# Three DMA pairs for two attention heads, and five loads moved ahead at the start of the output stage

## The chip, the cores and the metric

The kernel runs on one core of a Trainium2 chip. The metric is the device time of one execution in microseconds (us). Engines are named as in the profile: PE is TensorE, DVE is VectorE, ACT is ScalarE, POOL is GpSimd, SP is SyncE, which here only issues DMAs. Instructions run in order on each engine; between engines they wait for semaphores.

## The reference

Two blocks read the same input `x` (2048 tokens by 1024), and a gate mixes them:

```python
qkv = (x @ wqkv).reshape(B, S, 3, H, Dh).transpose(2, 0, 3, 1, 4)   # H = 32 heads, Dh = 32
scores = einsum("bhqd,bhkd->bhqk", q, k) * Dh ** -0.5
a = einsum("bhqk,bhkd->bhqd", softmax(scores), v).transpose(0, 2, 1, 3).reshape(B, S, D) @ wo

q = einsum("nd,dhc->nhc", x, w_q)              # 32 router heads, 2 x 128 wide
e = 8 * argmax(q[..., :128] @ k1.T) + argmax(q[..., 128:] @ k2.T)
b = sum over heads of gelu(x . u[e]) * v[e]    # K = 1: the softmax over one score is 1

g = sigmoid((x * gate_w).sum(-1))
out = g * a + (1 - g) * b
```

All of it is float32. The kernel splits many operands into a high and a low part and adds three products, so that a matmul keeps the precision.

## The kernel before, in words

The work stands in one hand-ordered program. Up to about 630 us come the projections, the router and the values. Then the 32 heads follow each other, and from about 1620 us the output product with `wo`.

**Attention.** A head `h` is 16 tiles of keys (`kt`). For each, PE makes scores for 128 keys and 2048 queries in a ring of seven PSUM banks (L1292), ACT writes their exponentials to an SBUF tile `P[h, kt]` of 128 x 2048 (L1301), and PE multiplies it with the values into `o` (L1313). The rows' sums for the softmax are formed apart: `presum` adds up the exponential tiles on DVE into `ACC[h]` (L1354, two instructions of half a tile each). Some tiles come in pairs: `accumulate` (L1343) adds one tile of a pair to the other with a DMA on POOL's queue, and `add_pair` and `merge` add the pair's sum to `ACC[h]` on DVE, the first one around the start of the next head. `pairs_of(h)` says which tiles are pairs: two pairs, (0, 2) and (8, 10), or three, with (4, 6) between. A head with three pairs has one addition less on DVE and one DMA of 1 MB more.

`p_tile` chooses the buffer of each exponential tile from the buffers that are left (13 places at first, 11 from the middle of head 19, 10 from head 29; two of them are kept for the end), always the one that its table `until` holds free earliest. That table gives the first tile of a pair 16 tiles of time, the second 10, and other tiles 5. ACT waits where the last reader of the buffer is not done. When the pairs change, the choice of buffers changes for every tile behind them. The copy of a finished head's output is `osb` (`finish`, L1390), one per head.

**The last head and the output.** The output is the product of the normed attention output with `wo`, 256 tokens (a chunk) at a time: `OD` holds the raw output of each group of four heads, `RD` the factors (gate over row sum), both in DRAM. `load_o` brings a chunk's part of `OD` into `V`, `load_rb` its factors, in a tile `P8` or `P9` (`rb` for chunk 0); `load_chunk` does both. Chunks 0 and 1 are done plainly (`wo_mm`, L1572); chunks 2 to 7 by `unit(n)`, a scheme of seven products of halves (`Halves.product`, L155). Its right-hand combinations of `wo`, T1 to T4, were made earlier and lie in DRAM as `TD`, a high and a low part of 1 MB each: `t0h`, `t0l` (T1), `t1h`, `t1l` (T2), `t2h`, `t2l` (T3), `t3h`, `t3l` (T4). `load_t(i, p, places)` loads part `p` of T(i+1). The DRAM tensor `t3l` is not the SBUF tile `t3l`: the tile holds `t2l`.

The last head's row sum goes a long way: PE sums (`sm`), ACT copies (`ssb`), SP stores it (`smd`), SP loads it spread out (`rr`), DVE takes the reciprocal (`norm_r`), SP stores it to `RD` (`rd`), and only then the last group's factors can be loaded: those of chunk 0 (`rb<-rd`), chunk 1 (`P<-rd`, small), chunk 2 and 3 (`P<-rd`, 256 KB each). All of these and the T loads stand on SP's queue; chunk 1's first part (`V<-od` x7, `P<-rd` x4) and `at` stand on POOL's. Between them PE does chunk 0 by `wo_mm(pa, 0, [kc])` for kc = 1 to 6, while `split_hi` and `split_lo` split `wo` out of `wo_raw0` to `wo_raw3`; the T parts are loaded over these tiles when they have been read.

Of the kernel before, what the change touches and what calls it, by code (L numbers as in the profile page):

```python
# [11 lines left out]
F32R = mybir.dt.float32r  # L12
# [5 lines left out]
S = 2048  # L18
D = 1024
H = 32  # L20
KC = D // 128
# [11 lines left out]
def gated_mha_peer_kernel(ctx, tc, xT, wqkv, wv, wo, wq, k12, ug, v, out):  # L33
# [46 lines left out]
    def dma(dst, src, queue=nc.sync):  # L80
        a, b = (ap.bitcast(F32) if ap.dtype == F32R else ap for ap in (dst, src))
        return queue.dma_start(a, b)  # L82
# [1068 lines left out]
    def pairs_of(h):  # L1151
        if h == H - 1:
            return (2, 4), (2, 6)
        if (h % 4 and h < 26) or h == H - 4:
            return (0, 2), (8, 10)
        return (0, 2), (4, 6), (8, 10)

# [63 lines left out]
    def raw_wo(kc):  # L1221
        i, j = divmod((kc - 1) % KC, 2)
        return wo_raw[i][:, j]
# [121 lines left out]
    def pair(h, i):  # L1345
        return P[h, pairs_of(h)[i][0]]
# [40 lines left out]
    def finish(h):  # L1387
        g, j = divmod(h, 4)
        o = wk.tile([128, 512], F32, name="osb")
        nc.scalar.activation(o, O.pop(h), AF.Copy)  # L1390
        dma(OD[g][32 * j:32 * j + 32, :].rearrange("d (q s) -> q d s", q=NQ), o)


    def norm_sums(h, ps, heads=1):
        g, j = divmod(h, 4)
        o = wk.tile([128, 512], F32, name="ssb")
        ins = nc.scalar.activation(o, ps, AF.Copy)
        for i in range(heads):
            dma(SMD[g][j + i:j + i + 1, :].rearrange("o (q s) -> (o q) s", q=NQ), o[32 // heads * i::32, :])
        return ins  # L1400


    def load_r(g):
        R[g] = wk.tile([128, 128], F32, name="rr", bufs=1)
        if g == G - 1:
            dma(R[g][:, :64], SMD[g].rearrange("j (b m) -> (j b) m", m=64))
        else:
            dma(R[g].rearrange("p (r m) -> p r m", r=2), SED[g][:2].rearrange("r j (b m) -> (j b) r m", m=64),
                nc.gpsimd if g == G - 2 else nc.sync)
# [13 lines left out]
    def load_o(n, k0, k1, queue=nc.sync):  # L1423
        if k0 == 0:
            OC[n] = vpool.tile([128, KC, W], F32, name="V")
        for kc in range(k0, k1):
            dma(OC[n][:, kc, :], OD[kc][:, n * W:(n + 1) * W], queue)

    def load_rb(n, k0, k1, js=range(4), queue=nc.sync):
        if k0 == 0 and js[0] == 0:  # L1430
            RB[n] = rb0 if n == 0 else wk.tile([128, KC, W], F32, name=f"P{8 + n % 2}", bufs=1)
        for j in js:
            src = RD[k0:k1, j:j + 1, n * W:(n + 1) * W].rearrange("g j s -> j g s")
            dma(RB[n][32 * j:32 * j + 32, k0:k1, :], src.to_broadcast([32, k1 - k0, W]), queue)

    def load_chunk(n, k0, k1, queue=nc.sync):
        load_o(n, k0, k1, queue)
        load_rb(n, k0, k1, queue=queue)
# [114 lines left out]
    fin = Pool("fin")  # L1553
# [41 lines left out]
    def split_hi(kc):  # L1595
        nc.scalar.activation(woh[kc], raw_wo(kc), AF.Copy)
        if kc < KC - 1:
            o = OC[0][:, kc, :]
            nc.vector.tensor_mul(o, o, RB[0][:, kc, :])
            nc.scalar.activation(OH[0][:, kc, :], o, AF.Copy)  # L1600

    def split_lo(kc):
        nc.vector.tensor_tensor(out=wol[kc], in0=raw_wo(kc),
                                in1=woh[kc].bitcast(F32), op=OP.subtract)
        if kc < KC - 1:
            nc.vector.tensor_tensor(out=OL[0][:, kc, :], in0=OC[0][:, kc, :],
                                    in1=OH[0][:, kc, :].bitcast(F32), op=OP.subtract)
# [3 lines left out]
    def load_t(i, p, part):  # L1611

        src, m = TD[i][p], HC // len(part)
        for j, place in enumerate(part):
            dma(place, src[:, m * j:m * j + m, :].rearrange("p k m -> p (k m)"))
        ht.b.setdefault(f"T{i + 1}", {})[p] = [place[:, k * 512:(k + 1) * 512] for place in part for k in range(m)]

    def raw_place(i):
        return [keep.tile([128, S], F32R, name=f"wo_raw{i}")]
# [18 lines left out]
    def split_o(n, k0, k1):  # L1638
        o = OC[n][:, k0:k1, :]
        nc.vector.tensor_mul(o, o, RB[n][:, k0:k1, :])  # L1640
        split(OH[n][:, k0:k1, :], OL[n][:, k0:k1, :], o)
# [7 lines left out]

    t3l = fin.tile([128, S], F32R, name="t3l")
    finish(H - 1)
    sm = pso.tile([128, 512], F32, name="o")
    list(rowsum(sm, *(P[H - 1, NT - i] for i in (1, 2)), ACC.pop(H - 1)))
# [4 lines left out]
    for kc in range(1, KC - 1):  # L1660
        split_hi(kc + 1)
        if kc == 1:
            norm_sums(H - 1, sm)
            load_r(G - 1)
            pso.close()
        split_lo(kc)
        wo_mm(pa, 0, [kc], False, False)
    split_lo(KC - 1)
# [1 line left out]
    norm_r(G - 1)  # L1670
    for n in range(2):
        load_chunk(n, KC - 1, KC)
        load_t(0, n, raw_place(n))
    load_t(2, 1, [t3l])
    OH[1] = zp.tile([128, KC, W], F32R, name="z1")
    OL[1] = wk.tile([128, KC, W], F32R, name="acc")
    split_o(1, 0, HC)
    load_chunk(2, 0, KC)
    load_t(1, 0, raw_place(2))
    ps_odd = Pool("ps_odd", space=PSUM)  # L1680
    for (i, half), ps in pa.items():
# [148 lines left out]
```

## Time and profile before

| what | us |
|---|---|
| runs: median (lowest to highest of 3) | 1808.1 (1807.08 to 1811.17) |
| the profiled execution | 1806.74 |
| its span in the profile | 1805.0 |
| PE busy over the span | 1795.3 (99%) |
| DVE busy | 1499.4 (83%) |
| ACT busy | 1217.7 (67%) |
| POOL busy | 273.6 (15%) |

A profile's busy time of PE includes ends that are modelled: matmuls overlap, and a PE that waits a little for ACT in every round still reads as full. The share of one engine over the whole span mixes stages with different limits, so the stages are looked at apart. In a row of the order of time stand start, duration, engine, line, operation, tiles (out<-in), their shapes and the number of instructions, and in brackets the idle time before them with what ended it. Engine names with a q are of the engine's queue: `SPq` is a DMA being issued, not being moved.

### The profile page before, as it was taken

What the parts mean: (1) busy time and instruction counts of PE and PEld (TensorE: products, weight loads), DVE (VectorE), ACT (ScalarE), POOL (GpSimd) and SP (SyncE); (2) the same over time, 40 slices, a digit from 0 to 9 for tenths busy, and PEclk for the clock granted to TensorE, in tenths of its full rate; (3) what the DMA queues carried; (4) which work ended last, traced back from release to release, by engine and by line L of the source; (5) the groups of instructions that cost most, each with busy time, mean ns of one, the idle gap of its engine ahead of it and who ended that gap; (6) DMA issues with size and microseconds to landing.
All of it is one profiled execution on the core that took longest, in us unless ns stands there. A gap on an engine that the chain in (4) does not pass through costs nothing.

```text
span 1805.0 us, 27885 instructions
## 1 busy us (share of the span) xinstructions
PE 1795.3 (99%) x10567; PEld 1135.2 (63%) x10567; DVE 1499.4 (83%) x1675; ACT 1217.7 (67%) x1608; POOL 273.6 (15%) x339
## 2 busy tenths in 40 slices
PE   9999999999999999999999999999999999999999
PEld 7777777788888754555454555454554545547787
DVE  7868776358987789999999999998999989895584
ACT  4434321211233399999999999999999999992221
POOL 0222000026401201111111111111111121211000
PEclk9999999999999999999999999999999999999999
DMA  6888888723238688899899999998998998977861
GB/s 241 237 285 255 276 258 294 261 79 107 82 125 278 227 200 173 173 186 205 175 209 189 197 201 192 194 189 178 196 213 180 206 218 191 201 153 204 282 180 65
DMA packets 132241, 359.04 MB, mean 199 GB/s; under 512 B 18484, under 2 KB 58564, under 8 KB 106936
## 3 DMA queue, kind: packets, MB, share of 16 engines
q1 hardware_dynamic: 90040, 190.61, 36.1%
q0 software_dynamic: 21904, 130.69, 35.9%
q10 hardware_dynamic: 20160, 35.92, 7.0%
q8 instruction: 84, 1.38, 0.3%
q14 instruction: 53, 0.43, 0.1%
HBM read 176.25 MB, written 86.09 MB: 145 GB/s over the span
## 4 chain that ended last, share of the span: by engine, by line
PE 95%; DMA 3%; SPq 1%; ACT 0%; DVE 0%; issue 0%; ACTq 0%; DVEq 0%
PE ring L1292 29%; PE o L1313 26%; PE bk L155 13%; PE bk L711 10%; PE pa L155 5%; PE bk L758 5%; PE bk L926 2%; PE bk L311 2%; PE bk L491 1%; PE bk L395 1%; DMA at<-atd 1%; SPq L82 1%; PE pa L1579 1%; DMA woh<-t3h 0%; DMA wraw<-in_wqkv 0%; DMA V<-od 0%
## 5 line engine op out<-in xcount | busy, mean ns | idle before, releaser
L1301 ACT ACTIVATE P<-ring 128x512 f32<-128x512 f32 (+3 forms) x991 | 812.9, 944 | 14.9 <-PE ring L1292 8.6
L1354 DVE TENSOR_TENSOR acc<-acc,P 128x1024 f32<-128x1024 f32 x424 | 488.3, 1217 | 18.9 <-ACT P L1301 18.9
L1313 PE MATMUL o<-P,V 128*32 128x512 f32 (+1 forms) x4072 | 417.5, 527 | 0.0
L1292 PE MATMUL ring<-Q,K 98*128 98x512 f32 x1024 | 269.0, 406 | 0.0
L1292 PE MATMUL ring<-z,z 98*128 98x512 f32 x1020 | 268.3, 406 | 0.1
L1292 PEld LDWEIGHTS ring<-Q,K 98*128 98x128 f32 x1024 | 182.8, 188 | 117.7 <-issue 37.0
L1292 PEld LDWEIGHTS ring<-z,z 98*128 98x128 f32 x1020 | 182.0, 188 | 115.6 <-ACT P L1301 39.6
L1313 PEld LDWEIGHTS o<-P,V 128*32 128x32 f32 x4072 | 112.3, 109 | 221.9 <-issue 201.9
L1354 DVE TENSOR_TENSOR rb<-rb,P 128x1024 f32<-128x1024 f32 x192 | 221.7, 1217 | 11.3 <-ACT P L1301 11.3
L1343 POOL DMA_DIRECT2D P<-P x57 | 51.8, 909 | 440.1 <-PE o L1313 134.0
L240 ACT ACTIVATE hi<-bk 128x512 fp32r<-128x512 f32 x40 | 23.7, 594 | 119.8 <-PE bk L711 100.9
L1301 ACT ACTIVATE wo_raw<-ring 128x512 f32<-128x512 f32 (+3 forms) x110 | 99.5, 988 | 1.0 <-PE ring L1292 0.2
L711 PE MATMUL bk<-xh,e 128*128 128x512 f32 x384 | 94.2, 394 | 0.0
L711 PE MATMUL bk<-xl,e 128*128 128x512 f32 x384 | 92.2, 389 | 0.0
L253 DVE TENSOR_TENSOR lo<-bk,hi 128x512 fp32r<-128x512 f32 x40 | 27.5, 689 | 69.2 <-ACT hi L240 67.1
L711 PEld LDWEIGHTS bk<-xh,e 128*128 128x128 f32 x384 | 71.0, 188 | 22.0 <-issue 3.4
L711 PEld LDWEIGHTS bk<-xl,e 128*128 128x128 f32 x384 | 72.1, 188 | 15.0
L101 DVE TENSOR_TENSOR e<-wraw,e 128x512 fp32r<-128x512 f32 (+3 forms) x64 | 54.6, 861 | 25.3 <-ACT e L100 24.4
L1301 ACT ACTIVATE vhl<-ring 128x512 f32<-128x512 f32 (+3 forms) x91 | 73.5, 893 | 0.9 <-PE ring L1292 0.6
L155 PE MATMUL bk<-xh,e 128*128 128x512 f32 x288 | 68.5, 393 | 0.0
L100 ACT ACTIVATE e<-wraw 128x512 fp32r<-128x512 f32 (+3 forms) x64 | 44.7, 705 | 34.1 <-DMA wraw<-in_wqkv 16.9
L155 PE MATMUL pa<-woh,acc 128*128 128x512 f32 x192 | 62.6, 390 | 2.4 <-ACT acc L100 2.1
(312 smaller groups left out, 2432.8 us busy)
## 6 DMA issues: line engine op xcount, KB each, us to landing
P<-P POOLq DMA_DIRECT2D x57, 1024.0 KB, 9.8
wqt<-in_wq SPq DMA_DIRECT2D x26, 1024.0 KB
wraw<-in_wqkv SPq DMA_DIRECT2D x30, 512.0 KB
acc<-acc POOLq DMA_DIRECT2D x20, 512.0 KB, 5.5
qdh<-hi ACTq DMA_DIRECT2D x32, 256.0 KB
qdl<-lo ACTq DMA_DIRECT2D x32, 256.0 KB
kdh<-hi ACTq DMA_DIRECT2D x32, 256.0 KB
kdl<-lo ACTq DMA_DIRECT2D x32, 256.0 KB
```

The costliest lines, as they stand in the source:

```text
L100: nc.scalar.activation(hi, src, AF.Copy)
L101: (on or nc.vector).tensor_tensor(out=lo, in0=src, in1=hi.bitcast(F32), op=OP.subtract)
L155: nc.tensor.matmul(ps, self.a[a][i][:, k, :], self.b[b][j][k], start=(not first and k == 0 and i == j == 0), stop=(k == HC - 1 and i == 1))
L311: nc.tensor.matmul(ps[32 * quad:32 * quad + 32, :], kpad[:, quad % 2, i, :], t[:, quad, :], start=(i == 0), stop=(i == 3))
L711: nc.tensor.matmul(ps, t[:, kc // HC, a, kc % HC], x_at(b, n, kc), start=first, stop=last)
L758: nc.tensor.matmul(ps, x_at(a, t // 4, kc)[:, tok], b, start=first, stop=last)
L926: nc.tensor.matmul(p, x_at(a, t // 4, kc)[:, tok], b, start=first, stop=last)
L1292: on_ring(nc.tensor.matmul(ring[:, i, :], K[:98, kt * 128:(kt + 1) * 128], Q[:98, qc * 512:(qc + 1) * 512], start=True, stop=True), i)
L1301: on_ring(nc.scalar.activation(P[h, kt][:, q0 * 512:(q0 + m) * 512].rearrange("p (a m) -> p a m", a=m), ring[:, i:i + m, :], AF.Exp, scale ...
L1313: nc.tensor.matmul(O[h][32 * qc:32 * qc + 32, c0:c1], Vt[g][:, kt, 32 * j:32 * j + 32], p[:, qc * 512 + c0:qc * 512 + c1], start=(kt == 0) ...
L1343: nc.gpsimd.dma_start(P[h, b], P[h, a], accum_op=OP.add)
L1354: nc.vector.tensor_add(out[:, c], a[:, c], b[:, c])
```

## The change

Four edits:

- `pairs_of`: of the heads below 26, a head has two pairs if it is odd, or if it is not a multiple of four and below 17. Heads 18 and 22, which had two pairs, get three; no other head changes.
- `t3l` (T3's low part) is loaded when its tile is made, ahead of the last head's `finish`, and not after chunk 1's last part.
- T1's two parts are loaded within the loop over chunk 0's kc, at kc = 3 and 5, when `wo_raw0` and `wo_raw1` have been split, and not after that loop.
- Chunk 2's factors are loaded ahead of its `OD` parts.

```diff
@@ pairs_of
-        if (h % 4 and h < 26) or h == H - 4:
+        if (h % 2 or (h % 4 and h < 17)) and h < 26 or h == H - 4:
             return (0, 2), (8, 10)
         return (0, 2), (4, 6), (8, 10)
@@ behind the last head
-    t3l = fin.tile([128, S], F32R, name="t3l")
+    load_t(2, 1, [fin.tile([128, S], F32R, name="t3l")])
     finish(H - 1)
@@ the loop over chunk 0's kc
             norm_sums(H - 1, sm)
             load_r(G - 1)
             pso.close()
+        if kc in (3, 5):
+            load_t(0, kc // 4, raw_place(kc // 4))
         split_lo(kc)
         wo_mm(pa, 0, [kc], False, False)
@@ behind it
     norm_r(G - 1)
     for n in range(2):
         load_chunk(n, KC - 1, KC)
-        load_t(0, n, raw_place(n))
-    load_t(2, 1, [t3l])
     OH[1] = zp.tile([128, KC, W], F32R, name="z1")
     OL[1] = wk.tile([128, KC, W], F32R, name="acc")
     split_o(1, 0, HC)
-    load_chunk(2, 0, KC)
+    load_rb(2, 0, KC)
+    load_o(2, 0, KC)
     load_t(1, 0, raw_place(2))
```

What this does to the order of the instructions is seen at three places.

POOL's queue in head 18 and at the start of head 19, before. L1343 is an accumulating DMA: `P7` and `P8` are head 18's tiles 0 and 2, `P0` and `P2` its tiles 8 and 10, and the last row is head 19's first pair. The other rows are the folds of row sums of earlier heads.

```order
L1343 DMA P7_9515<-P8_9530 128x2048
L1378 DMA sed3_91<-sed3_91 32x2048
L1375 DMA sed4_92<-acc_9101 32x2048
L1371 DMA rb0_5211<-rb0_5211 64x2048
L1343 DMA P0_9633<-P2_9661 128x2048
L1378 DMA sed3_91<-sed3_91 16x2048
L1371 DMA rb0_5211<-rb0_5211 32x2048
L1343 DMA P6_9756<-P8_9771 128x2048
```

The same place now:

```order
L1343 DMA P7_9515<-P8_9530 128x2048
L1378 DMA sed3_91<-sed3_91 32x2048
L1375 DMA sed4_92<-acc_9101 32x2048
L1371 DMA rb0_5211<-rb0_5211 64x2048
L1343 DMA P1_9565<-vhl_9598 128x2048
L1343 DMA P0_9629<-P2_9658 128x2048
L1378 DMA sed3_91<-sed3_91 16x2048
L1371 DMA rb0_5211<-rb0_5211 32x2048
L1343 DMA P8_9755<-P3_9770 128x2048
```

Tiles 4 and 6 (`P1`, `vhl`) are a pair now, and the buffers behind them are others: head 19's first pair lies in `P8` and no longer in `P6`.

ACT at the start of head 20, before: from its second tile (`P8`) to its fifth (`vhl`). `P6` was the buffer of head 19's first pair, whose last reader is a DVE addition at the very end of head 19's work; that is the wait for DVE in the row of `P6`.

```order
L1301 ACTIVATE P8_10006<-ring_5230 128x512 [waits DMASW2_49,PE_49]
L1301 ACTIVATE P8_10006<-ring_5230 128x1536 [waits PE_49]
L1301 ACTIVATE P1_10013<-ring_5230 128x512 [waits DVE_49,PE_49]
L1390 ACTIVATE osb_10030<-o_9808 128x512 [waits DMAHW1_49,PE_49]
L1301 ACTIVATE P1_10013<-ring_5230 128x512 [waits PE_49] x3
L1301 ACTIVATE P6_10043<-ring_5230 128x2048 [waits DVE_49,PE_49]
L1301 ACTIVATE vhl_10047<-ring_5230 128x1024 [waits PE_49]
```

The same place now, where `P8` is the buffer of head 19's first pair:

```order
L1301 ACTIVATE P9_10005<-ring_5230 128x512 [waits DVE_49,PE_49]
L1301 ACTIVATE P9_10005<-ring_5230 128x1536 [waits PE_49]
L1301 ACTIVATE P2_10012<-ring_5230 128x512 [waits DVE_49,PE_49]
L1390 ACTIVATE osb_10029<-o_9805 128x512 [waits DMAHW1_49,PE_49]
L1301 ACTIVATE P2_10012<-ring_5230 128x512 [waits PE_49] x3
L1301 ACTIVATE P0_10042<-ring_5230 128x2048 [waits DVE_49,PE_49]
L1301 ACTIVATE P8_10046<-ring_5230 128x1024 [waits DVE_49,PE_49]
```

The pair's buffer is reused one tile later, for the fifth tile. The fourth, `P0`, was head 19's tile 11, which DVE adds well ahead of the pair.

SP's queue between the last head and chunk 2, before. `wo_raw` are the places of T1's parts, the row `P` is chunk 1's last factors (32x256), and the last row begins chunk 2.

```order
L82 DMA rr<-smd_87 128x64
L82 DMA rd<-rr 128x64
L82 DMA V<-od_78 128x256
L82 DMA rb_5211<-rd 32x256 x4
L82 DMA wo_raw_13097<-t0h 128x2048
L82 DMA V<-od_78 128x256
L82 DMA P_12968<-rd 32x256 x4
L82 DMA wo_raw_13104<-t0l 128x2048
L82 DMA t3l<-t2l 128x2048
L82 DMA V<-od_71 128x256
```

The same queue now; the last row is chunk 2's factors (32x8x256).

```order
L82 DMA t3l<-t2l 128x2048
L82 DMA od_78<-osb 4x32x512
L82 DMA smd_87<-ssb 4x512
L82 DMA rr<-smd_87 128x64
L82 DMA wo_raw_13022<-t0h 128x2048
L82 DMA wo_raw_13058<-t0l 128x2048
L82 DMA rd<-rr 128x64
L82 DMA V<-od_78 128x256
L82 DMA rb_5211<-rd 32x256 x4
L82 DMA V<-od_78 128x256
L82 DMA P_12967<-rd 32x256 x4
L82 DMA P_13110<-rd 32x8x256 x4
```

The three loads of 1 MB have gone from between the reciprocals and chunk 2: `t3l` stands ahead of the store of the last head's output (`od`), `t0h` and `t0l` between the load of the sums (`rr`) and the store of their reciprocals (`rd`).

## The prediction

> **What bounds the kernel now.** I read the busy time by stretches first, then the waits of TensorE (PE) and ScalarE (ACT), then the order of time around each wait. Columns of the first rows: stretch in us, then busy time of PE, PE's weight loads, VectorE (DVE), ACT and POOL, the granted clock, the share of the DMA engines, GB/s.
>
> ```profile
> 1200.00:1400.00 200.00, 200.00 (x1395) 100.57 (x1389) 187.36 (x170) 196.35 (x248) 32.45 (x41) 1.00 0.91 191
> ```
> ```profile
> 1668.00:1694.00 26.00, 22.85 (x99) 18.04 (x98) 13.72 (x19) 6.29 (x11) 0.00 (x0) 1.00 0.96 295
> 1694.00:1760.00 66.00, 66.00 (x291) 54.49 (x292) 51.34 (x77) 16.92 (x29) 0.00 (x0) 1.00 0.71 211
> ```
>
> In the attention stage ACT is busy 98% of the time and DVE 94%; PE reads full because its ends are modelled. So an edit there saves time only where ACT stands still. In the output stage the second row is the one that matters: from 1668 to 1694 ACT and DVE are mostly idle, PE lacks 3.15 of 26 us, and the DMA engines are 96% busy. The waits there, from 1618 to the end (waiter, what ended the wait, us, times, longest):
>
> ```profile
> PE pa L155 <- ACT acc L100: 2.1, 1, 2.1
> PE pa L155 <- ACT osb L1729: 0.8, 1, 0.8
> PE pa L155 <- DVE acc L101: 0.3, 1, 0.3
> ```
>
> These three are everything PE waits for between the last head and the tail. The change can win this, and what ACT loses in attention, and little else.
>
> **Part one: heads 18 and 22 get a third DMA pair.** Of 32 heads only these two change. Each trades one tile addition on DVE (two instructions) for one accumulating DMA of 1 MB on POOL's queue.
>
> ```profile
> DMA to landing us min/median/max: 7.1/10.1/14.8
> ```
>
> What counts here is whether ACT waits less; its waits for DVE in the whole stage, 640 to 1580 us, and the row between them:
>
> ```profile
> ACT P L1301 <- DVE acc L1354: 0.6, 1, 0.6
> ACT vhl L1301 <- PE ring L1292: 0.6, 3, 0.2
> ACT P L1301 <- DVE rb L1354: 0.5, 1, 0.5
> ```
>
> Twice, then. One row per head is the copy of the head's output (`osb`), so its starts give the period:
>
> ```profile
> 1217.90 0.67 ACT L1390 ACTIVATE osb<-o 128x512 f32<-128x512 f32 x1
> ```
> ```profile
> 1248.88 0.67 ACT L1390 ACTIVATE osb<-o 128x512 f32<-128x512 f32 x1
> ```
> ```profile
> 1251.62 1.88 ACT L1301 ACTIVATE P<-ring 128x2048 f32<-128x2048 f32 x1 [0.59 <-DVE acc L1354]
> 1253.39 2.00 ACT L1301 ACTIVATE vhl<-ring 128x1024 f32<-128x1024 f32 x3
> ```
> ```profile
> 1280.31 0.62 ACT L1390 ACTIVATE osb<-o 128x512 f32<-128x512 f32 x1
> ```
> ```profile
> 1373.22 0.60 ACT L1390 ACTIVATE osb<-o 128x512 f32<-128x512 f32 x1
> ```
> ```profile
> 1375.80 2.85 ACT L1301 ACTIVATE P<-ring 128x1536 f32<-128x1536 f32 x3 [0.51 <-DVE rb L1354]
> ```
> ```profile
> 1404.58 0.65 ACT L1390 ACTIVATE osb<-o 128x512 f32<-128x512 f32 x1
> ```
>
> From 1217.90 to 1248.88 is 30.98 us; the two periods with a stall are 1280.31 - 1248.88 = 31.43 and 1404.58 - 1373.22 = 31.36. So the stalls cost 0.45 + 0.38 = 0.83 us, both at the start of heads 20 and 24, each the head after three heads in a row with two pairs. DVE there:
>
> ```profile
> 1221.91 2.36 DVE L1354 TENSOR_TENSOR acc<-vhl,wo_raw 128x1024 f32<-128x1024 f32 x2 [1.99 <-ACT wo_raw L1301]
> ```
> ```profile
> 1240.09 11.43 DVE L1354 TENSOR_TENSOR acc<-acc,P 128x1024 f32<-128x1024 f32 x10
> ```
>
> The ten additions take 1.14 us each, so the change relieves DVE of 4 x 1.14 = 4.6 us, beside ACT's work, where it saves nothing by itself. DVE's run ends at 1251.52, and the exponential at 1251.62 starts right behind it. The program's order names the tie: ACT's fourth tile of head 20 overwrites the tile that head 19's first pair was summed into, whose last reader is the last of those additions. The changed order puts a tile with a much earlier reader in fourth place, and the pair's tile in fifth, some 1.8 us later (1253.39 against 1251.62). Head 22 has its tiles in that order now, behind a head with three pairs and one with two as heads 20 and 24 will be, and shows no wait. DVE cannot be relied on to be earlier: it waited 1.99 us at 1221.91, so it was not behind, and the 2.3 us taken from head 18 fall partly into such a wait. The gain comes from the place of the tile, not from the load. I take both stalls away: -0.83 us. Bounds: -0.83 (no more is there), and +2 if the new rotation makes four stalls of the size seen, 0.45 each. The accumulates themselves I cost at nothing: an accumulate is issued two tiles behind its source, and the planner gives that source's buffer away ten tiles behind it, so 8 x 30.98 / 16 = 15.5 us cover a landing of 10.1, at most 14.8; heads 20 and 24 carry three pairs with no ACT wait on a DMA. POOL first waits until PE has read the tile; where that takes more than the 0.7 us left over, the longest landing would show on ACT, one for one.
>
> **Part two: 3 MB of TD are loaded earlier.** SP issues these in order, and the program gives its DMAs eight semaphores in turn, so that each also waits for the landing of the one eight before it.
>
> ```profile
> 1644.69 0.42 SPq L82 DMA_DIRECT2D wo_raw<-t0h  x1
> ```
> ```profile
> 1648.36 0.34 SPq L82 DMA_DIRECT2D t3l<-t2l  x1
> 1650.13 6.63 SPq L82 DMA_DIRECT2D V<-od  x8
> ```
> ```profile
> 1660.32 1.80 SPq L82 DMA_DIRECT2D z<-t2h  x1
> ```
> ```profile
> 1665.46 13.16 SPq L82 DMA_DIRECT2D V<-od  x8
> 1678.80 2.75 SPq L82 DMA_DIRECT2D P<-rd  x4
> ```
> ```profile
> SPq L82 <- DMA z<-t2h: 2.8, 1, 2.8
> ```
>
> Eight issues of chunk 3's `V` take 13.16 us because SP waits for `t1h`, `t2h` and `t1l` to land; only then come chunk 3's factors, at 1678.80. PE pays at both ends:
>
> ```profile
> 1675.49 0.47 PE L155 MATMUL pa<-z,s 128*128 128x512 f32 x1 [0.76 <-ACT osb L1729]
> 1675.80 0.40 PE L155 MATMUL pa<-t3l,s 128*128 128x512 f32 x1
> 1676.03 0.62 PE L155 MATMUL pa<-z,s 128*128 128x512 f32 x2
> ```
> ```profile
> 1690.81 2.36 DVE L1625 TENSOR_TENSOR V<-V,P 128x1024 f32<-128x1024 f32 x2 [9.26 <-DMA P<-rd]
> ```
> ```profile
> 1692.80 0.50 PE L155 MATMUL pa<-woh,acc 128*128 128x512 f32 x1 [2.10 <-ACT acc L100]
> ```
>
> The matmul at 1675.49 reads `t2h` (tile `z`); I put its wait down to that landing rather than to the `osb` copy named, which has nothing that it reads. The one at 1692.80 needs chunk 3's first factor, which DVE could not make before 1690.81, and the 0.29 us behind it is the same factor's low part. Two matmuls take 0.62 us and one 0.39 (2 x 0.39 less an overlap), so starts are 0.23 apart and each wait costs its idle time plus 0.16: 0.76 + 2.10 + 0.29 + 3 x 0.16 = 3.63 us.
>
> After the change `t0h`, `t0l` and `t3l` no longer stand ahead of chunk 2 and chunk 3. At 295 GB/s (the second stretch above) 3.1 MB are 10.7 us; at 1692.80 only 2.3 us are missing. DVE stands idle 9.26 us before 1690.81, so it can take the factor that much earlier. Chunk 2's factors also go ahead of its `V` on SP, and the `V` loads then wait for their landing; one DVE product needs both, and PE did not wait for it, so I take nothing for the order. I take -3.63 for the whole; bounds -3.63 (the list of waits holds no more) and 0 (if `t2h` and chunk 3 are paced by something else). Nothing is late next by the stretch from 1694, where PE is full. That the transfers have room where they go is seen in the DMA share:
>
> ```profile
> 1618.00:1625.00 7.00, 7.00 (x49) 3.27 (x52) 7.00 (x7) 3.61 (x5) 3.02 (x6) 1.00 0.20 42
> ```
> ```profile
> 1636.00:1645.00 9.00, 9.00 (x41) 7.44 (x41) 5.51 (x7) 1.06 (x1) 0.00 (x0) 1.00 0.26 71
> ```
>
> ```profile
> 1616.02 9.16 DVE L1354 TENSOR_TENSOR acc<-acc,P 128x1024 f32<-128x1024 f32 x8
> ```
>
> `t3l` now waits for DVE and PE to be done with the tile it overwrites; in the changed order that is the fourth of these eight additions, at 1616.02 + 9.16 / 2 = 1620.6, so it runs in the stretch at 20%. `t0h` and `t0l` wait for two splits of the weights and go behind `rr<-smd`, mostly into the stretch at 26%. These waits hold SP: the store of the last head's output stands behind `t3l`, the reciprocals' store behind `t0l`. Their data share the engines with POOL's loads of chunk 1, and PE is not far behind those:
>
> ```profile
> 1640.16 1.22 DVE L1640 TENSOR_TENSOR V<-V,P 128x1024 f32<-128x1024 f32 x1
> ```
> ```profile
> 1641.42 1.06 ACT L100 ACTIVATE z<-V 128x1024 fp32r<-128x1024 f32 x1 [5.98 <-DVE V L1640]
> ```
> ```profile
> 1645.56 1.07 PE L1572 MATMUL pa<-woh,z 128*128 128x512 f32 x4
> ```
> ```profile
> P<-rd POOLq DMA_DIRECT2D x4, 224.0 KB, 7.6
> ```
> ```profile
> out<-rb POOLq DMA_DIRECT2D x4, 256.0 KB, 12.3
> ```
>
> PE uses `z` at 1645.56 and ACT has it at 1642.48: 3.1 us of slack. POOL's stores beside `t1h` and `t2h` took 12.3 us for 256 KB, its loads on quieter engines 7.6 us for 224 KB, per byte 1.42 times as long. So chunk 1's loads may land 0.42 x 7.6 = 3.2 us later, or by the whole difference 12.3 - 7.6 = 4.7. Of that 3.1 is slack: 0.1 to 1.6 us would be PE's. I take nothing, since only the tail of these loads meets `t0h`; the bound is +1.6.
>
> [...]
>
> **Sum.** -0.83 - 3.63 = -4.46 us. The profiled execution took 1806.74 us (span 1805.0 and 1.7 around it), 1.4 below the median of the runs, 1808.1. So 1802.3 for a profile like it, and 1803.6 for the median.
>
> **Rivals.** (a) *Only the output stage gains.* The rotation of tiles trades one stall for another in attention: heads 20 and 24 show that a stall costs 0.4. Then -3.63 to -2.8: 1804.5 to 1805.3. (b) *Attention alone gains, or little does:* chunk 3 is paced by its own factors, which took from 1678.80 to 1690.81, 12 us, for 1 MB. Issued before 1678.80 - 2.3 = 1676.5 they free PE, later PE waits again; with POOL's loads late as well (+1.6) no more than 0.83 to 2 us are gained: about 1806.7. Against it: SP reaches them late for the sake of the three loads that have gone. (c) *Slower:* `rr<-smd` is held up, by `t3l` ahead of it and by `t0h` and `t0l` beside it. DVE takes its reciprocal and only then chunk 1's product (1640.16), so behind the 3.1 us of slack PE stalls one for one. 2 MB at 71 to 295 GB/s are 30 to 7 us. From a delay of 3.1 + 4.5 = 7.6 us on the kernel is slower than before; at 12 us it takes 1812.5. Against it: `rr<-smd` is issued ahead of `t0h` on the same queue.
>
> **Chances.** Forecast 0.55, (a) 0.2, (b) 0.15, (c) 0.1. From no change a measurement of this kernel tells 0.2%, 3.6 us. Faster by more needs 1804.5: the forecast, and a part of (a), 0.62; within 0.2% the rest of (a) and (b), 0.27; slower by more 0.11. The range runs from 1801.8 (the whole gain and the runs' lower edge of 1.0 below the median, with 0.8 for a run faster still) to 1808.0 (b with a wait more and the same spread).
>
> **What would show it.** Right: periods of 31.0 us for heads 20 and 24 and no ACT wait on DVE; chunk 3's factors issued before 1674 and DVE's first product of it no longer ended by a DMA; PE without a wait of over 0.3 us from 1640 to 1700; the stretch 1668 to 1694 shorter by 3.6 us. Wrong: a PE wait near 1645 (POOL's loads or `rr` late), a wait that stays at chunk 3 with the factors' DMA ahead of it, or ACT waits for DVE or a DMA in heads 19 to 25.

## The result and the profile after

The median of 16 runs is 1805.4 us (1802.9 to 1808.6), against 1808.95 us (1806.9 to 1811.8) for the kernel before in 16 runs beside it: a ratio of 0.998 with a 95% interval of 0.9973 to 0.9988, or 3.55 us less. The forecast was 4.46 us less. The two profiled executions are nearer to each other: 1806.74 and 1804.75 us, spans 1805.0 and 1803.0.

Attention first. The starts of the head's output copy (`osb`) in the changed kernel:

```profile
1218.17 0.68 ACT L1390 ACTIVATE osb<-o 128x512 f32<-128x512 f32 x1
...
1249.14 0.68 ACT L1390 ACTIVATE osb<-o 128x512 f32<-128x512 f32 x1
...
1280.12 0.62 ACT L1390 ACTIVATE osb<-o 128x512 f32<-128x512 f32 x1
...
1373.08 0.60 ACT L1390 ACTIVATE osb<-o 128x512 f32<-128x512 f32 x1
...
1404.05 0.65 ACT L1390 ACTIVATE osb<-o 128x512 f32<-128x512 f32 x1
```

The two long periods are now 1280.12 - 1249.14 = 30.98 and 1404.05 - 1373.08 = 30.97 us. All that ACT waits for from 640 to 1580 us is PE:

```profile
ACT P L1301 <- PE ring L1292: 6.1, 31, 0.3
ACT vhl L1301 <- PE ring L1292: 0.6, 3, 0.2
ACT wo_raw L1301 <- PE ring L1292: 0.2, 1, 0.2
```

In the output stage PE's waits from 1616 us to the end, and the stretch that was 22.85 of 26 us busy:

```profile
PE pa L155 <- ACT acc L100: 1.6, 1, 1.6
PE pa L155 <- DVE acc L101: 0.3, 1, 0.3
```
```profile
1668.00:1694.00 26.00, 24.14 (x106) 19.36 (x105) 13.87 (x20) 6.29 (x11) 0.00 (x0) 1.00 0.97 295
```

The wait for `t2h` is gone. The wait for chunk 3's first factor is still there: 1.6 us instead of 2.1, with the small one behind it as before. First two rows of the kernel before, the reciprocal on DVE and the issue of `t1h`:

```profile
1639.36 0.55 DVE L1416 RECIPROCAL rr<-rr 128x64 f32<-128x64 f32 x1 [1.07 <-DMA rr<-smd]
...
1658.77 1.46 SPq L82 DMA_DIRECT2D wo_raw<-t1h  x1
```

What SP issues up to there in the changed kernel, and the reciprocal and chunk 3's product on DVE:

```profile
1620.15 0.34 SPq L82 DMA_DIRECT2D t3l<-t2l  x1
...
1634.69 0.33 SPq L82 DMA_DIRECT2D rr<-smd  x1
1635.12 0.38 SPq L82 DMA_DIRECT2D wo_raw<-t0h  x1
...
1642.56 0.32 SPq L82 DMA_DIRECT2D rd<-rr  x1
...
1648.99 3.71 SPq L82 DMA_DIRECT2D P<-rd  x8
1652.80 10.58 SPq L82 DMA_DIRECT2D V<-od  x8
1663.42 0.49 SPq L82 DMA_DIRECT2D wo_raw<-t1h  x1
...
1665.72 10.69 SPq L82 DMA_DIRECT2D V<-od  x8
1676.58 2.88 SPq L82 DMA_DIRECT2D P<-rd  x4
```
```profile
1641.72 0.55 DVE L1416 RECIPROCAL rr<-rr 128x64 f32<-128x64 f32 x1 [3.98 <-DMA rr<-smd]
...
1688.75 2.36 DVE L1625 TENSOR_TENSOR V<-V,P 128x1024 f32<-128x1024 f32 x2 [7.78 <-DMA P<-rd]
```

Chunk 3's factors are issued 2.2 us earlier than before (1678.80), and DVE's product starts 2.1 us earlier (1690.81). PE itself arrives earlier by the two gains ahead of it, so only 0.5 us of its wait is won. The reciprocal starts at 1641.72 instead of 1639.36, and `t1h` is issued at 1663.42 instead of 1658.77.

In the traces the gains are 0.87 us in attention (first to last `osb` copy 960.41 us, before 961.28), 0.92 for `t2h`, 0.53 for chunk 3; the changed execution began its attention 0.30 us later for no reason of the change. Together -0.87 - 0.92 - 0.53 + 0.30 = -2.02, the difference of the spans (1805.0 and 1803.0). The other 1.5 us of the medians are not in these two traces; the experiments find a cost that most runs of the kernel before have, and its profiled one not.

### The profile page after: what moved, and what is told of

It is laid out like the page before. It is cut to its first block, busy times and chain, and to the rows that moved or that the text cites. A ratio compares the mean times of both kernels' runs of the same rounds, so it can differ in the third digit from the quotient of the medians.

```text
span 1803.0 us, 27887 instructions
## 1 busy us (share of the span) xinstructions
PE 1795.0 (100%) x10567; PEld 1136.7 (63%) x10567; DVE 1495.4 (83%) x1671; ACT 1217.9 (68%) x1608; POOL 275.4 (15%) x341
## 4 chain that ended last, share of the span: by engine, by line
PE 96%; DMA 3%; SPq 1%; ACT 0%; DVE 0%; issue 0%; ACTq 0%; DVEq 0%
PE ring L1292 29%; PE o L1313 26%; PE bk L155 13%; PE bk L711 10%; PE pa L155 5%; PE bk L758 5%; PE bk L926 2%; PE bk L311 2%; PE bk L395 1%; PE bk L491 1%; SPq L82 1%; DMA wo_raw<-t1l 1%; DMA P<-rd 1%; PE pa L1579 1%; DMA smd<-ssb 0%; DMA woh<-t3h 0%
## 5 line engine op out<-in xcount | busy, mean ns | idle before, releaser
L1354 DVE TENSOR_TENSOR acc<-acc,P 128x1024 f32<-128x1024 f32 x418 | 482.2, 1218 | 26.5 <-ACT P L1301 26.5
L1354 DVE TENSOR_TENSOR rb<-rb,P 128x1024 f32<-128x1024 f32 (+1 forms) x188 | 217.4, 1218 | 11.6 <-ACT P L1301 11.6
L1343 POOL DMA_DIRECT2D P<-P x60 | 55.3, 922 | 427.5 <-PE o L1313 147.8
L1301 ACT ACTIVATE vhl<-ring 128x512 f32<-128x512 f32 (+3 forms) x100 | 79.6, 881 | 0.9 <-PE ring L1292 0.6
```

The costliest lines, as they stand in the source:

```text
L1301: on_ring(nc.scalar.activation(P[h, kt][:, q0 * 512:(q0 + m) * 512].rearrange("p (a m) -> p a m", a=m), ring[:, i:i + m, :], AF.Exp, scale ...
L1343: nc.gpsimd.dma_start(P[h, b], P[h, a], accum_op=OP.add)
L1354: nc.vector.tensor_add(out[:, c], a[:, c], b[:, c])
```

## The experiments

The theory to start from: chunk 3's wait stayed since SP came to its factors too late, because the eight semaphores held it, or because `t0h` and `t0l` delayed the reciprocals. The rival was that the factor loads are slow by themselves. Later kernels split "slow by themselves" further. All results (a kernel's ratio is to the kernel before on the same chip, whose median was 1809.65 to 1809.95 there; the changed kernel was timed on another chip, so it is compared with the others by the ratios as well; the last two columns are PE's wait for chunk 3's first factor in the profile, and how many of the timed runs had a mean granted clock of 1.000). A profile is of one execution, and not always a middling one: it is the slowest of the timed runs for the pairs alone, the pairs and t3l alone and the eight matmuls more, and the fastest for the loads alone and chunk 2's order alone. So the column of waits is a sample of one, and medians and ratios weigh more:

| kernel | median us | ratio, 95% interval | wait us | clock 1.000 |
|---|---|---|---|---|
| before (runs beside the experiments) | 1809.65 to 1809.95 | 1 | 2.10 | 14 of 79 |
| changed | 1805.4 | 0.9973 to 0.9988 | 1.57 | 8 of 16 |
| pairs alone | 1808.96 | 0.9985 to 1.0004 | 3.23 | 1 of 10 |
| loads alone | 1810.95 | 0.9997 to 1.0016 | 2.28 | 1 of 10 |
| t0 behind the loop | 1803.62 | 0.9955 to 0.9980 | none | 6 of 6 |
| chunk 2's V first | 1808.68 | 0.9987 to 1.0006 | 3.23 | 0 of 10 |
| chunk 3's factors from the weights | 1802.27 | 0.9946 to 0.9974 | none | 5 of 5 |
| chunk 3's factors on POOL's queue | 1810.8 | 0.9990 to 1.0013 | none (t2h 4.33) | 1 of 10 |
| chunk 3's factors first | 1803.7 | 0.9954 to 0.9979 | none | 6 of 6 |
| pairs and t3l alone | 1807.4 | 0.9979 to 0.9998 | 3.3 | 0 of 10 |
| t0 behind, factors first twice | 1803.31 | 0.9949 to 0.9977 | none | 5 of 5 |
| chunk 2's order alone | 1808.71 | 0.9985 to 1.0004 | 1.61 | 4 of 10 |
| eight matmuls more | 1808.4 | 0.9983 to 1.0001 | 2.89 | 7 of 11 |
| one row per partition | 1802.33 | 0.9948 to 0.9973 | none | 6 of 6 |

**The pairs alone.** The kernel before with the condition of heads 18 and 22.

```diff
-        if (h % 4 and h < 26) or h == H - 4:
+        if (h % 2 or (h % 4 and h < 17)) and h < 26 or h == H - 4:
```

> The pairs of heads 18 and 22 alone, all loads as before. My theory of the parts: heads 20 and 24 have periods of 30.97 us (before 31.43 and 31.36), ACT shows no wait for DVE from 640 to 1580 us, and the output stage is the old one: PE waits 0.8 (t2h), 2.1 and 0.3 us, chunk 3's factors are issued 2.1 to 2.3 us ahead of the old place relative to nothing but the stage's start. Time 0.8 us below before, which the timing cannot tell from no change. Rival (the rotation of tiles only moves the stall): other heads show periods of 31.4 and the time is that of before, or above it.

First to last `osb` copy takes 960.52 us (1621.50 - 660.98), 0.76 less than before, and no wait of ACT for DVE is left: the attention term is this edit's. The median is 0.7 us below the kernel before (1808.96 against 1809.66), as the attention term says, though the timing cannot tell that from no change. The profiled execution, the slowest of the ten, took 1810.6 us, with a wait of 3.23 us at chunk 3. Behind it the granted clock is half (first row the kernel with the pairs alone, from 1694 to 1700; second row the same stretch of the kernel before, whose wait was 2.10):

```profile
1694.00:1700.00 6.00, 5.74 (x13) 4.24 (x14) 4.42 (x7) 1.47 (x3) 0.00 (x0) 0.50 1.05 389
```
```profile
1694.00:1700.00 6.00, 6.00 (x27) 4.80 (x28) 4.37 (x8) 1.26 (x2) 0.00 (x0) 1.00 1.05 385
```

13 matmuls in the time of 27: some 3 us are lost there on top of the wait. No term of the prediction had this price. The longer wait does not come from an earlier PE. PE reached chunk 3 at 1694.26 - 3.23 = 1691.03, before at 1692.80 - 2.10 = 1690.70, since its attention began 0.54 us later and `t2h` held it for 1.27 us instead of 0.76; but DVE's product starts at 1692.27 instead of 1690.81. Why the loads were later in this execution is not shown.

**The load edits alone.** The changed kernel with the old condition for the pairs.

```diff
-        if (h % 2 or (h % 4 and h < 17)) and h < 26 or h == H - 4:
+        if (h % 4 and h < 26) or h == H - 4:
```

> The load edits alone, the pairs as before. If the parts add up: stalls at the start of heads 20 and 24 as before (periods 31.4 us), output stage as in the changed kernel: no wait on t2h, PE waits 1.5 to 1.7 us for chunk 3's first factor and 0.3 behind it, 1.4 us won in the stage; time 1.4 us below before by the trace. Rival: the attention edit shifts the stage's transfers against each other, and without it the wait at chunk 3 differs by more than 0.3 us.

The stalls of heads 20 and 24 are back (0.60 and 0.54 us). `t2h`'s wait is gone as expected, but in the fastest of ten runs the wait at chunk 3 is 2.28 us, 0.7 above the changed kernel, and the clock falls behind it:

```profile
1692.00:1696.00 4.00, 3.74 (x11) 2.79 (x10) 2.44 (x5) 1.26 (x2) 0.00 (x0) 0.57 1.04 400
```

So the rival was right, and the two parts are not independent: the loads with the pairs stand at 0.998, without them at 1.0006, and the pairs alone at 0.9994. SP's waits from 1616 to 1650 us, of this kernel and then of the changed one, show a link that the order of the program suggests, and that no run tests alone: `t3l` waits for all of DVE's eight additions here and for four of them there, and is issued at 1624.87 instead of 1620.15.

```profile
SPq L82 <- DMA smd<-ssb: 11.0, 1, 11.0
SPq L82 <- DVE acc L1354: 9.3, 1, 9.3
```
```profile
SPq L82 <- DMA smd<-ssb: 6.6, 1, 6.6
...
SPq L82 <- DVE acc L1354: 4.7, 1, 4.7
```

`smd<-ssb`, issued at 1627.59 (there 1627.48), then lands 4.4 us later, behind `t3l`, and `rr` is issued at 1639.16. By themselves the loads won nothing that the timing can tell (1.0006).

**t0 behind the loop.** The changed kernel with that edit undone.

```diff
-        if kc in (3, 5):
-            load_t(0, kc // 4, raw_place(kc // 4))
...
     for n in range(2):
         load_chunk(n, KC - 1, KC)
+        load_t(0, n, raw_place(n))
```

> The changed kernel with t0h and t0l back behind the loop (the second edit of the loads undone, t3l still early). Theory that the two loads in front of the reciprocals delay the chain: rr lands within 5.3 us of its issue instead of 7.0, the reciprocal starts 2.0 to 2.4 us earlier relative to the start of the stage, and so does everything that waits for the reciprocals' store (chunk 1's last group, chunk 2's factors). If that delay is what kept chunk 3 waiting, chunk 3's factors are issued before 1675 and PE's wait of 1.57 us falls to 0 to 0.3. Rival (chunk 3 is paced by the loads between and by its own factors): t0h and t0l, 2 MB, stand ahead of chunk 2 again, chunk 3's factors are issued no earlier than 1676, PE's wait stays at 1.2 to 2.1 us, and a wait for t2h comes back (up to 0.8). Time by the first 1.6 us below the changed kernel, by the second 0 to 1.5 above.

The first theory held: 1803.6 us (ratio 0.9968 against 0.998), and a granted clock of 1.000 in all six runs, where the changed kernel has it in 8 of 16. The intervals of the two ratios overlap a little, up to 0.9980 and from 0.9973. The reciprocal starts 2.4 us earlier than in the changed kernel and chunk 3's factors are issued 1.5 us earlier, 0.1 us past the bound set:

```profile
1639.32 0.55 DVE L1416 RECIPROCAL rr<-rr 128x64 f32<-128x64 f32 x1 [1.51 <-DMA rr<-smd]
...
1675.10 2.66 SPq L82 DMA_DIRECT2D P<-rd  x4
```

What PE still waits for is

```profile
PE pa L155 <- DVE acc L101: 0.2, 1, 0.2
```

In the seven profiles with `t0h` and `t0l` early and behind `rr` (the changed kernel and six experiments) the reciprocal starts between 1639.0 and 1641.8 us, in the seven others (the kernel before among them) between 1639.0 and 1639.6. So these loads cost the chain of the reciprocals 0 to 2.4 us, from run to run (with the loads alone, part of it is `rr`'s own late issue); by the medians this part of the change was a loss of some 2 us.

**Chunk 2's V first.** The changed kernel with the last edit undone.

```diff
-    load_rb(2, 0, KC)
-    load_o(2, 0, KC)
+    load_chunk(2, 0, KC)
```

> The changed kernel with the last edit undone: chunk 2's V is issued ahead of its factors again. Theory that the order of the two decides nothing, since one product needs both and eight semaphores hold the second of the two to the landing of the first: chunk 2's first product within 1 us of 1664.3, chunk 3's factors within 1 us of 1676.6, PE's wait for chunk 3 between 1.2 and 2.0 us, time within 0.5 us of the changed kernel. Rival (slow factors in front hold V, t1h, t2h and t1l back by the eight semaphores, since the eight issues of V took 10.58 us behind them): with V in front t1h is issued 2 to 4 us earlier than 1663.4, chunk 3's factors 2 to 4 us earlier than 1676.6, and PE's wait for chunk 3 goes to 0; time 1.5 to 2 us below the changed kernel.

Both expectations fell: V first is worse by 3.3 us (0.9997 against 0.998), with a wait of 3.23 us and none of ten runs at the full clock. SP in this kernel:

```profile
1654.17 1.86 SPq L82 DMA_DIRECT2D P<-rd  x4
1656.08 1.75 SPq L82 DMA_DIRECT2D wo_raw<-t1h  x1
...
1664.15 14.32 SPq L82 DMA_DIRECT2D V<-od  x8
1678.65 1.81 SPq L82 DMA_DIRECT2D P<-rd  x4
```

With V first, chunk 2's factors are issued at 1654.2 instead of 1650.9 and run beside `t1h`, `t2h` and `t1l`; DVE's product of them starts at 1667.67 (1664.34 for the first half in the changed kernel). Eight issues of chunk 3's V then take 14.32 us instead of 10.69, and its factors are issued 2.1 us later. The order of the two loads, which the prediction costed at nothing, carries most of the changed kernel's gain, with the other edits in place.

**Chunk 3's factors from the weights.** Four loads of the same size and run length, whose rows no two partitions share. Chunk 3 is left without its factors by that.

```diff
-    load_chunk(3, 0, KC)
+    load_o(3, 0, KC)
+    RB[3] = wk.tile([128, KC, W], F32, name="P9", bufs=1)
+    for j in range(4):
+        src = wo[32 * j:32 * j + 32, :].rearrange("p (k d) -> p k d", k=KC)
+        dma(RB[3][32 * j:32 * j + 32, :, :], src[:, :, :W])
```

> The changed kernel, where chunk 3's factors are read from rows that no other partition reads (the weights), as many loads of the same size and of the same 1 KB runs; the factors are left out of chunk 3 by that. Theory that a factor load is slow because 32 partitions read the same row (in the changed kernel 159 GB/s at a DMA share of 1.00 from 1680 to 1689, where V and TD move 411 at 1.01): issued at the same 1676.6, they land 4 to 7 us later instead of 12, DVE's first product starts before 1684.5, PE has no wait over 0.3 us, all runs show a granted clock of 1.000, time 2 to 4 us below the changed kernel. Rival (the loads are slow because they are short runs, or because t3h and t3l stand behind them on the same engines, or the issue at 1676.6 is what counts): landing after 10 to 13 us as before, PE's wait stays at 1.2 to 2.0 us.

Issued at 1676.38, they let DVE start at 1684.82, 0.3 us past the bound set and 3.9 us earlier than in the changed kernel. No wait of PE is left. The last two columns are the share and the rate of the DMA engines, from 1680 to 1683 us, in the changed kernel and here:

```profile
1680.00:1683.00 3.00, 3.00 (x15) 2.49 (x14) 0.97 (x2) 0.17 (x1) 0.00 (x0) 1.00 0.95 104
```
```profile
1680.00:1683.00 3.00, 3.00 (x15) 2.49 (x14) 0.00 (x0) 0.00 (x0) 0.00 (x0) 1.00 1.00 228
```

About equally busy, they move 104 GB/s in the one and 228 in the other, whatever else is under way included.

**One row per partition.** This takes the tensor and the repetition apart: the same tensor of reciprocals is read, each partition its own row. Chunk 3 is not normed by this either.

```diff
-    load_chunk(3, 0, KC)
+    load_o(3, 0, KC)
+    RB[3] = wk.tile([128, KC, W], F32, name="P9", bufs=1)
+    for j in range(4):
+        dma(RB[3][32 * j:32 * j + 32, :, :], RD.rearrange("g j (a m) -> (g j a) m", m=W).rearrange("(k p) m -> p k m", k=KC))
```

> The changed kernel, where chunk 3's factors are read from the same tensor of reciprocals and in 1 KB runs as before, four loads of 256 KB, but within one load each partition reads a row of its own instead of 32 partitions the same one (the values are then not chunk 3's factors, so its normalisation is left out). It takes apart what the reading from the weights changed at once: the tensor and the repetition. Theory that the repetition makes a factor load slow: 200 GB/s or more from 1680 us until they have landed (changed kernel 88 to 134), product of chunk 3 before 1686, no PE wait over 0.5 us, granted clock 1.000 in all runs, 1801.5 to 1803.5. Rival (the tensor is what is slow: small, 256 KB, and written shortly before): 90 to 140 GB/s, product at 1688 or later, PE's wait 1.2 to 2.0 us, clock 0.999 in some runs, 1804.5 to 1806.

```profile
1677.87 1.81 SPq L82 DMA_DIRECT2D P<-rd  x4
```
```profile
1684.88 2.36 DVE L1625 TENSOR_TENSOR V<-V,P 128x1024 f32<-128x1024 f32 x2 [3.98 <-DMA P<-rd]
```
```profile
1680.00:1683.00 3.00, 3.00 (x15) 2.49 (x14) 0.90 (x2) 0.10 (x1) 0.00 (x0) 1.00 1.07 232
```

The rate is that of the weights, from the same small tensor, so the repetition is what is slow. These loads were not fast on idler engines either: with the pairs alone, chunk 3's factors, issued from 1679.59 on, are used at 1692.27, and from 1688 to 1690 the DMA share is 0.53 and the rate 117 GB/s, with all else under way. With a row per partition the issue is 1.3 us later than in the changed kernel, and still the product starts 3.9 us earlier and PE has no wait. SP's late issue, the prediction's cause, was not the only one: the four factor loads take 12.2 us from their first issue to DVE's product (1676.58 to 1688.75) where 7.0 (1677.87 to 1684.88) are enough for the same bytes.

**Chunk 3's factors on POOL's queue.**

```diff
-    load_chunk(3, 0, KC)
+    load_rb(3, 0, KC, queue=nc.gpsimd)
+    load_o(3, 0, KC)
```

> The changed kernel with chunk 3's factors on POOL's queue, behind its four stores, so that they don't wait for SP's turn: issued at 1661.5 to 1664.5 instead of 1676.6. Theory that the wait at chunk 3 is SP's order: the product of chunk 3 starts before 1684, PE's wait of 1.57 us goes, granted clock 1.000 in all runs, time 2 to 4 us below the changed kernel. Rival (the slow factors then run beside t1h, t2h and t1l and hold those up, as chunk 2's factors did in the kernel with V in front, where they took 13.5 us): t2h lands after 1674.0 and PE waits for it 0.5 to 3 us, or t1h and t1l after 1676.8 and 1679.5; the wait moves and the time is that of the changed kernel within 1 us, or above.

The rival held. Issued at 1662.01, the factors run beside `t1h`, `t2h` and `t1l`, and PE waits for `t2h`, at half the clock afterwards (the first two rows are its waits):

```profile
PE pa L155 <- DMA z<-t2h: 4.3, 1, 4.3
PE pa L155 <- DVE acc L101: 1.2, 1, 1.2
```
```profile
1680.00:1684.00 4.00, 3.75 (x10) 2.97 (x11) 2.59 (x5) 1.78 (x3) 0.00 (x0) 0.57 0.86 314
```

One of ten runs kept a clock of 1.000, and it took 1802.2 us where the others took 1809.0 to 1812.6. It has no profile; that `t2h` landed in time there is likely and not shown. From POOL's queue the slow loads were issued 1.7 us ahead of `t2h` (1663.69), which PE could read at 1680.25, 16.6 us after its issue; in the next kernel they stand behind `t2h` on SP's queue, and PE read it without a wait at 1673.81, 11.4 us after its issue (1662.38). The factors were also issued 2.1 us earlier here than there, and queue and time were not taken apart.

**Chunk 3's factors first, on SP's queue.**

```diff
-    load_chunk(3, 0, KC)
+    load_rb(3, 0, KC)
+    load_o(3, 0, KC)
```

> The changed kernel with chunk 3's factors ahead of its V on SP's queue, as the change does for chunk 2. Theory that slow loads should be issued first: factors issued at 1665.7 to 1669, landed by 1680 although they run beside t1h, t2h and t1l; V goes out behind them and lands by 1684, so the product starts 4 us or more before 1688.75, PE's wait of 1.57 us goes, clock 1.000, time 2 to 4 us below the changed kernel. Rival: t2h is held up by the factors beside it (it is needed at 1674.0) and PE waits 0.5 to 3 us there; or the eight semaphores hold V to 1683 and later and the wait at chunk 3 stays.

Issued at 1664.14, behind `t1h`, `t2h` and `t1l` on the same queue, they don't hold those up. The product starts at 1683.88, and only a wait of another kind is left:

```profile
PE pa L155 <- DVE rb L161: 1.1, 1, 1.1
```

1803.7 us. Its V is issued late, over 13.74 us, as the rival said, and still lands in time.

**Pairs and t3l alone.** The kernel before with the new condition for the pairs and `t3l` loaded ahead of the last head's end.

```diff
-    t3l = fin.tile([128, S], F32R, name="t3l")
+    load_t(2, 1, [fin.tile([128, S], F32R, name="t3l")])
...
-    load_t(2, 1, [t3l])
```

> The kernel before with the pairs and t3l early, t0h and t0l behind the loop, chunk 2's V in front: with the runs so far it completes the square of t0's place and chunk 2's order. If the two act by themselves (t0 behind the loop won 1.8 us with the factors first, factors first won 3.3 with t0 in the loop), this one stands 1.8 us below the kernel with t0 in the loop and V first: 1806.9. Rival (t3l's 1 MB, gone from between chunk 2's loads, is all that the output stage gained): 1804 to 1805.5, PE's wait at chunk 3 under 1.5 us. Second rival (t3l alone brings nothing without the order): PE waits 2 to 3.3 us for chunk 3 as before, 1808 to 1809. In any case a wait of 2.2 us or more goes with a granted clock near 0.5 for 3 to 7 us behind it, one under 2.1 us with 1.00.

1807.4 us, within 0.5 us of the additive estimate: 2.4 below the kernel before, although the wait at chunk 3 is 3.3 us in the profile and no run keeps a clock of 1.000. With V first, `t0h` and `t0l` in the loop cost 1.3 us (1808.68), with the factors first 1.8 (1805.4 against 1803.6); the factors first win 3.3 or 3.8.

**T0 behind the loop and the factors first for chunks 2 and 3.** The edits of the two kernels above joined.

> The changed kernel with t0h and t0l back behind the loop and the factors first for chunk 3 as well as for chunk 2: the two edits that each took the wait at chunk 3 away (1803.6 and 1803.7 us). If that wait and the slow clock behind it are all that is left to win there, the two together win no more than the better of them: 1803 to 1804, all runs at a granted clock of 1.000, no PE wait for DVE's product of chunk 3. Rival (t0 behind the loop runs beside chunk 2's factors and pushes t2h or chunk 3's V back): a wait of 0.5 us or more at t2h or at chunk 3, 1804 to 1806.

As expected they add nothing to one another: 1803.3 us, 0.9963 of the kernel before, within the spread of either alone. All three medians are below the changed kernel's; which of the three is best, these runs don't tell.

**Chunk 2's order alone.** The kernel before with the factors ahead of V.

```diff
-    load_chunk(2, 0, KC)
+    load_rb(2, 0, KC)
+    load_o(2, 0, KC)
```

> The kernel before with one edit alone: chunk 2's factors issued ahead of its V. Pairs, t0h, t0l and t3l as before. Theory that this order is what the changed kernel gains from (t3l early with V first stood at 1807.4 to 1808.7, with the factors first at 1803.6 to 1805.4): PE's wait at chunk 3 under 2.1 us in most runs, granted clock mostly 1.000, 1805 to 1807.5. Rival (without t3l and t0 out of the way the order gives nothing): wait of 2.1 to 3.3 us, clock 0.998 to 0.999 in most runs, 1808.5 to 1810; t2h may come later too, since t1h and t2h are issued behind 10 us of V.

In between: the wait falls to 1.61 us in the profile and four of ten runs keep the clock, but the median is 1808.7, which the timing cannot tell from the kernel before. `t1h` is issued at 1665.84 here, behind `t0h`, `t0l` and `t3l`. The kernel with t0 behind the loop has `t0h` and `t0l` in the same place, issues `t1h` at 1661.26 and takes 1803.6 us. It differs from this one by the pairs and by `t3l`, so what the order needs is in those two, and not in t0.

**Eight matmuls more.** The kernel before, where PE fills 1.8 us ahead of chunk 3's first product with work of no use.

```diff
+    def fill(ps):
+        for _ in range(4):
+            av_mm(2, 1, 1, ps, True, True)
...
-        p1 = ht.product("P1")
+        p1 = ht.product("P1", fill if n == 3 else None)
...
-                                     start=(not first and k == 0 and i == j == 0),
+                                     start=((not first or first.__name__ == "fill") and k == 0 and i == j == 0),
```

> The kernel before with eight more matmuls (1.8 us) ahead of chunk 3's first product, in the bank that the product then starts anew: they take no data from chunk 3 and fill most of PE's wait. The loads are untouched, so the product can start no earlier. Theory that a wait of 2.2 us and more sets the clock to half for 2 to 7 us and that this costs the kernel before 2 to 3 us in most of its runs: the wait falls to 0.3 to 1.5 us, granted clock 1.000 in all runs, median 1806 to 1807.5, that is 1.5 to 3 us below the kernel before although PE does more. Rival (the low clock is not from the wait, or costs nothing): clock 0.998 to 0.999 in most runs as before, and a median of 1809 or above.

7 of 11 runs keep a clock of 1.000, against 3 of 21 of the kernel before beside it, and the median is 1.5 us lower with more work on PE. The theory asked for more, 1.000 in all runs and 1806 to 1807.5 us, and the ratio's interval reaches 1.0001: the gain is likely and not settled. The profiled execution, the slowest, is one in which the factors were issued 2.8 us later than in the profile of before (1681.63) and the wait was long nevertheless:

```profile
1696.58 0.50 PE L155 MATMUL pa<-woh,acc 128*128 128x512 f32 x1 [2.89 <-ACT acc L100]
```
```profile
1698.00:1704.00 6.00, 6.00 (x21) 4.77 (x20) 4.37 (x8) 1.26 (x2) 0.00 (x0) 0.72 0.99 343
```

The clock falls behind the wait in every profile whose wait is 2.28 us or more. That a shorter wait spares it, this kernel supports by its share of undisturbed runs.

## Why the prediction was right, and where it was not

The sign and the range held. Step by step:

- *Attention, -0.83 us:* right. -0.87 in the changed kernel, -0.76 with the pairs alone, the stalls back without them. The place of the tile was the reason given; the load of DVE was not tested apart from it.
- *The accumulates at nothing:* right. No wait of ACT for a DMA or POOL is in the rows above.
- *`t2h`, -0.92 us:* right in size; gone in the changed kernel and with the loads alone. With the pairs alone the profile puts the wait of the same matmul down to `t2h` itself, as the prediction read it.
- *Chunk 3, -2.71 us (2.10 + 0.29 + 0.32):* wrong; 0.53 was won in the trace. The step that failed is "at 1692.80 only 2.3 us are missing", with the sentence that DVE "can take the factor that much earlier": it priced what was removed ahead of chunk 3 at 295 GB/s and took the factors' own 12 us as given. They were to be issued before 1674 and were at 1676.58. The 10.7 us of bytes did not turn into an earlier `t1h`: it was issued 4.7 us later, with the reciprocal 2.4 us late and V's eight issues, now behind chunk 2's slow factors, taking 10.58 us instead of 6.63. What rival (b) named, that chunk 3 is paced by its own factors, is as true as the late issue: with the repetition taken out, PE has no wait even at an issue of 1677.87, and with the slow loads it has almost none at 1675.10. Undoing either was enough. A wait that stays at chunk 3 with the factors' DMA ahead of it was one of the prediction's own signs of being wrong.
- *Chunk 2's order, "nothing":* wrong; 3.3 us by the kernel that undoes it. It decides which loads the slow ones run beside.
- *`t0h` and `t0l`:* rival (c) named the mechanism, and it is there, at 0 to 2.4 us on the reciprocal instead of the 7.6 it needed. It fell within the slack at 1645, as no PE wait there shows, but it passed on to chunk 3; undone, the kernel is at 1803.6. POOL's loads cost PE nothing, as forecast.
- *From profile to median:* the prediction carried over 1.4 us as a constant. It is not one: the kernel before ran at a mean clock of 1.000 in its profile and in 14 of 79 runs beside the experiments. With the changed kernel half of the runs keep it. So the median gained 3.55 us where the traces gained 2.0. Two errors, a chunk 3 term too large by 2.2 us and a price left out, partly cancel: that the gain came within 0.9 us of the forecast is in part luck.

## What to carry to other kernels

Before pricing an earlier issue by bytes over bandwidth, take the load's own time from issue to use, and ask what is slow about it: four loads in which 32 partitions read the same rows took 12 us where the same bytes from separate rows took 7. Put such a load ahead of what can wait (chunk 3's factors ahead of its V: 1803.7 us instead of 1805.4), and judge an order of loads by what they will run beside (chunk 2's factors beside its V, not beside `t1h`, `t2h` and `t1l`: 1805.4 instead of 1808.7). And price a wait of PE beyond its length: here the clock stayed at 1.00 behind 2.10 us and fell to half behind 2.28, and by estimate the fall cost 1.7 or 3.4 us more.

## What the runs showed of the hardware

The granted clock fell to half behind PE's longer waits. In the profiles, waits of 1.57 us (the changed kernel), 1.61 (chunk 2's order alone) and 2.10 (the kernel before) left it at 1.00; waits of 2.28 (the loads alone), 2.89 (eight matmuls more), 3.23 (the pairs alone and chunk 2's V first), 3.3 (the pairs and t3l alone) and 4.33 us (chunk 3's factors on POOL's queue) were each followed by a stretch at 0.50. The rows above give its length: 4 us at a mean of 0.57 are 3.4 us at a half, and so are 6 us at 0.72. It is 3.4 us in four of the six traces and twice that, 6.8, in the other two: 2 us at 0.92, 6 at 0.50 and 4 at 0.94 with the pairs alone, 2 at 0.97, 6 at 0.50 and 2 at 0.83 with the pairs and t3l alone. By estimate, half of such a stretch is lost: one such wait costs 1.7 or 3.4 us on top of its length, and over 1805 us that is a mean clock of 0.999 or 0.998. The runs show such values: of the 79 of the kernel before, 14 at 1.000 have a median of 1807.5 us, 50 at 0.999 1809.8, 15 at 0.998 1811.1, though the longer waits themselves are in these figures too.

The stretch did not begin at the same distance from the wait. With the pairs and t3l alone it began 2.4 us after PE stopped, with chunk 2's V first 5.1 us after, when PE had been at work again for 1.9. What sets its start and its length is not shown.

While four loads whose 32 partitions read the same 1 KB rows were under way, the DMA engines moved 104 GB/s at a share of 0.95, and 117 at 0.53 with the pairs alone; with the same loads from separate rows of the same tensor it was 232 at 1.07. Why the repeated reads are slow was not tried.
